# Earlier pooling of v, earlier requests for k, and a reordered first batch in a one-core attention and MLP kernel

## The chip, the cores and the metric

The kernel runs on one core of a Trainium2 chip. The metric is device time in microseconds of one execution. A core has five engines that each take their instructions in order and meet through semaphores: TensorE (PE in the profile, with weight loads as PEld), VectorE (DVE), ScalarE (ACT), GpSimd (POOL) and SyncE (SP), which here issues nearly all DMAs.

## The reference

Two parts, in float32. First an attention in which k and v are averaged over groups of 8 positions, so that 576 queries meet 72 pooled keys; then an MLP with a sine activation over all 8 x 576 = 4608 rows.

```
k_p = k.reshape(B, H, Sp, pool, D).mean(axis=3)        # B, H, S, D = 8, 8, 576, 64; pool = 8, Sp = 72
v_p = v.reshape(B, H, Sp, pool, D).mean(axis=3)
scores = scale * q @ k_p.T ; scores -= max
attn = exp(scores) / (sum + 1e-9)
x = (attn @ v_p) as [4608, 512]
h = x @ w_in                                            # 512 x 2048
g = h + sin(alpha*h)**2 / (alpha + 1e-9)
out = g @ w_out                                         # 2048 x 512
```

## The kernel before

Both matrix products of the MLP are done by Strassen's scheme (seven products for eight). Stage one (`hidden`, matmul at line 770) makes h and g for 512 rows at a time: nine units u = 0 to 8, each of 28 slots, a slot being one of the seven products of one quarter of the columns (four matmuls, 8 records in the trace). g goes to DRAM. Stage two (`outputs`, line 1103) reads g back and makes the output, two levels of Strassen deep.

The attention of batch b = u + 1 is laid between the slots of unit u. `carry(u)` is the written-out plan: `at(slot, f, ...)` puts a call before that slot. All orders are by hand: each engine executes its instructions in the order in which the Python calls issue them, and a DMA request is an instruction in SP's queue. Each DMA has one of eight semaphores in turn, so at most eight are in flight.

What the attention of one batch does in unit u (1 to 6):

- `load_v` (slot 6): two DMAs of 512 KB for the main part of v (512 of 576 rows per head) into a buffer `kvin`, four of 64 KB for the rest into `vr`.
- `two_scores`, `two_shifts` (slots 3 to 6): scores, maximum, subtraction. `exp` on ScalarE (slots 8 to 10). `norm(i)` for four query tiles (slots 9 to 12): a sum and a reciprocal on VectorE, and on GpSimd a multiplication (line 343).
- `turn(i)` (slots 12, 13): VectorE transposes 32 x 32 blocks of the weights into a tile `tr`. `move` (slot 14): sixteen DMAs of 88 or 92 KB (line 487) carry `tr` into `aM`, transposed tile by tile.
- `pool_v` (slot 12): GpSimd adds v's eight neighbours by three halvings (`pool_rows`, line 118), main part, then the rest, then a masked copy (line 137).
- `load_k` (slots 12 and 14, one half of the heads each): one DMA of 576 KB into a `kvin` buffer, and at once its pooling on GpSimd. `kvin` has two buffers, used in turn by v's main part and the two halves of k: a half of k can be requested only when the buffer's last content is pooled. SP's order in slot 14 is: eight moves, second half of k, eight moves.
- `all_values` (slot 25): 44 matmuls (lines 568, 581) of the moved weights with pooled v. They need all moves. `turn_q` (line 209) transposes queries of a later batch into the same `tr`.

Unit 0 has a plan of its own: `load_k(2)` for both halves at slot 17, moves at slot 19, `all_values` at slot 26.

Before slot 0 stands `first_batch`, the attention of batch 0 done in another way, since nothing is there to hide it. Head pairs hp = 0 to 3 go one after the other: `k_head` and `k_last` pool the keys by a matmul with a matrix of ones (`twos`) and copy them from PSUM to `kb2` (`k_last` makes the last 8 of the 72 keys of all heads, from a separately loaded `k_rest`, whose partial sums VectorE adds at lines 148 and 150); `q_head` transposes queries; `products_head` makes scores; `soft_shift`, `soft_exp`, `norm_head` the softmax, the last with two multiplications at line 416 on the engine that it is given; `a_head` transposes the weights, `values` multiplies them with v. `sum_v_rest` and `sum_v_rows` pool v by matmuls (lines 179, 189), copied out by VectorE (line 180) and ScalarE (line 190). `fill(n)` issues n matmuls of ones whose result nobody reads, and line 943 one more of 512 columns. `refine` is four small VectorE operations on the factors of the activation. `self.psum(shape, i)` is PSUM bank i, of eight.

Of the kernel before, what the change touches and what calls it, by code (L numbers as in the profile page):

```python
# [16 lines left out]
OP = mybir.AluOpType  # L17
PSUM = bass.MemoryType.PSUM

P = 128  # L20
POOL = 8
# [19 lines left out]
class Kernel:  # L41
# [61 lines left out]
    def load_k(self, b, e):  # L103

        Sp, D, NP = self.Sp, self.D, self.NP
        m = Sp // 3
        t = self.kvp.tile([P, 2048], F32, name="kvin")[:NP * m, 0:3 * POOL * D]
        self.nc.sync.dma_start(out=t, in_=self.k[b, NP * e:NP * e + NP].rearrange("h (p x) d -> (h p) (x d)", x=3 * POOL))
        if b not in self.kp:
            self.kp[b] = self.ap.tile([NP * m, 3, 2, D], F32, name="kp")  # L110
        t, out = t.rearrange("p (j x) -> p j x", j=3), self.kp[b][:, :, e, :]
        self.pool_rows(t, out)

    def pool_rows(self, t, out):

# [4 lines left out]
    def load_v(self, b):  # L120

        nc, D, H = self.nc, self.D, self.H
        vm, vz = self.vp[b] = self.ap.tile([P, H // 2, D], F32, name="vm", bufs=2), self.ap.tile([P, H // 2, D], F32, name="vz", bufs=2)
        t = self.kvp.tile([P, 2048], F32, name="kvin")[:].rearrange("p (h x) -> p h x", h=4)
        x = self.kvp.tile([P, POOL * D], F32, name="vr", bufs=1)[:]
        for s in range(2):
            nc.sync.dma_start(out=t[64 * s:64 * s + 64],
                              in_=self.v[b, 4 * s:4 * s + 4, 0:4 * P, :].rearrange("h (p t) d -> p h (t d)", t=POOL))
        for s in range(2):
            for c in range(2):  # L130
                r = 64 * s + 32 * c
                nc.sync.dma_start(out=x[r:r + 32], in_=self.v[b, 4 * s:4 * s + 4, 4 * P:, :].rearrange("h (k t) d -> h k (t d)", t=POOL))

        def pool():
            self.pool_rows(t, vm[:])
            self.pool_rows(x, x[:, 0:D])
            nc.gpsimd.tensor_tensor(out=vz[:], in0=x[:, 0:D].unsqueeze(1).to_broadcast([P, H // 2, D]),
                                    in1=self.mask[:].unsqueeze(2).to_broadcast([P, H // 2, D]), op=OP.mult)
        self.pool_v = pool

    def load_k_rest(self, x, out):

        D = self.D
        self.nc.sync.dma_start(out=x, in_=self.k[0, :, 4 * P:, :].rearrange("h (r t) d -> h r (t d)", t=4))
        self.k_rest = out

        def add():
            self.nc.vector.tensor_tensor(out=x[:, 0:2 * D], in0=x[:, 0:2 * D], in1=x[:, 2 * D:4 * D], op=OP.add)
            both = lambda y: y.unsqueeze(1).to_broadcast([P, 2, D])
            self.nc.vector.tensor_tensor(out=out.rearrange("p (u d) -> p u d", u=2), in0=both(x[:, 0:D]), in1=both(x[:, D:2 * D]), op=OP.add)  # L150
        return add

    def load_k_heads(self, hp, dma, eng):
# [25 lines left out]
            nc.tensor.matmul(ps[32 * hp:32 * hp + 32], self.eights[:], self.v_rows[1][:, 2 * hp:2 * hp + 2], start=True, stop=True)  # L179
        nc.vector.tensor_tensor(out=self.vp[b][1][:, 0:2], in0=ps, in1=self.mask[:, 0:2].unsqueeze(2).to_broadcast([P, 2, self.D]), op=OP.mult)  # L180

    def sum_v_rows(self, b, g, i):

        nc = self.nc
        ps = self.psum([P, 2, self.D], i)
        for t in range(4):
            for s in range(2):
                h = 4 * g + 2 * s
                nc.tensor.matmul(ps[64 * s:64 * s + 64], self.twos[:], self.v_rows[0][:, h:h + 2, t, :], start=(t == 0), stop=(t == 3), skip_group_check=True)
        nc.scalar.copy(out=self.vp[b][0][:, 2 * g:2 * g + 2], in_=ps)  # L190
# [37 lines left out]
    def attention(self, b):  # L228
# [125 lines left out]

        def k_last():

            ps = self.psum([P, H, Sp - 64], 4)
            nc.tensor.matmul(ps.rearrange("p h k -> p (h k)"), self.k_rest, self.twos[:], start=True, stop=True)
            nc.vector.tensor_copy(out=self.kb2[:, :, 64:Sp], in_=ps)

# [18 lines left out]

        def products_head(hp):  # L380

            at = 3 if hp % 2 else 5
            self.pair[hp] = ps = self.PS[:, at:at + 2, 0:4 * Sp].rearrange("p u (x k) -> p u x k", x=4)
            for e in range(2):
                for tp in range(2):
                    q = self.qt_tiles(b)[:, hp, 2 * e + tp, :]
                    for r in (0, 64):
                        for u in range(2):
                            s = slice(64 * u, 64 * u + 64)
                            nc.tensor.matmul(ps[r:r + 64, u, 2 * e + tp, :], q[s, r:r + 64], self.kb2[s, 2 * hp + e, :], start=True, stop=True)  # L390
# [133 lines left out]
        def values(hps, banks, n, d):  # L524

            ps = [self.psum([P, 4 * P], i) for i in banks]
            parts = [value_parts(hp, False) for hp in hps]
            for o, (main, _) in zip(ps, parts):
                for e, (w, x) in enumerate(main):
                    nc.tensor.matmul(o[64 * e:64 * e + 64], w, x, start=True, stop=False, skip_group_check=True)  # L530
            for o, (_, (w, x)) in zip(ps, parts):
                nc.tensor.matmul(o, w.rearrange("p e d -> p (e d)"), x, start=False, stop=True, skip_group_check=True)
            if d == 0:
                self.bt[0] = self.home(3, [P, 4, 2, TH])
            turned = [o.rearrange("p (t j) -> p j t", t=4) for o in ps]
            for i in range(n):
                for hp, o in zip(hps, turned):
                    to_x(o, hp, 0, 512 // n * (i + 1), 512 // n * i)
            for kk, o in enumerate(turned):
                y = self.bt[0][:, 0, kk] if d else self.xT[0][:, kk, 0:TH]  # L540
                f = lambda x: x.rearrange("p (j t) -> p j t", t=4)
                nc.vector.scalar_tensor_tensor(out=f(self.bt[0][:, d, kk]), in0=o[:, TH // 4:TH // 2, :], scalar=1.0 / POOL, in1=f(y),  # L542
                                               op0=OP.mult, op1=OP.subtract)

        def values_rest(banks):

# [312 lines left out]
    def first_batch(self):  # L859
# [9 lines left out]
        self.new_q(0)  # L869
        self.load_alpha(self.hp.tile([P, P], F32, name="s", bufs=1)[:])  # L870
        self.load_q_heads(0, 0, 2, nc.scalar)
        add_k = [self.load_k_heads(0, nc.sync, nc.vector)]
        one = self.sm.tile([P, 1], F32, name="one")
        nc.scalar.activation(out=one[:], in_=self.ident[:, 0:1], func=AF.Sqrt)

        def fill(n):

            for _ in range(n):
                nc.tensor.matmul(self.PS[:, 0, 3 * P:4 * P], self.full[:], self.full[:], start=True, stop=True)  # L879
        fill(5)  # L880
        self.turn_alpha()
        refine = self.root()
        nc.scalar.activation(out=one[:], in_=one[:], func=AF.Exp)
# [6 lines left out]
        self.a4 = self.last[:64, 0:512].rearrange("p (j s k) -> p j s k", j=4, s=2)  # L890
        self.z4 = self.last[:64, 512:640].rearrange("p (hp x k) -> p hp x k", hp=4, x=4)
        nc.gpsimd.memset(self.z4, 0.0)
        add_rest = self.load_k_rest(h[1][:, 576:832], far[1][:, 1024:1152])
        for hp in range(1, 4):
            add_k.append(self.load_k_heads(hp, nc.sync, nc.vector if hp < 2 else nc.gpsimd))
            self.load_q_heads(0, 2 * hp, 2 * hp + 2)
# [4 lines left out]
        A.new_a()  # L901
        fill(3)
        A.k_head(0)
        add_rest()
        A.q_head(0)
        A.k_last()
        for f in add_k[1:]:
            f()
        fill(3)
        A.products_head(0)  # L910
        A.k_head(1)
        A.q_head(1)
        A.soft_shift(0)
        A.soft_exp(0)
        refine()
        fill(3)
        A.products_head(1)
        A.k_head(2)
# [2 lines left out]
        A.soft_exp(1)  # L921
        A.norm_head(0, nc.gpsimd)
        A.norm_head(1, nc.vector)
        fill(2)
        A.products_head(2)
        A.k_head(3)
        A.q_head(3)
        self.sum_v_rest(0, 0)
        A.soft_shift(2)
        self.sum_v_rows(0, 0, 2)  # L930
        A.a_head(0, (1, 7, 0))
        self.combine_w_in(0, (0,), nc.gpsimd)
        A.products_head(3)
        A.soft_exp(2)
        A.soft_shift(3)
        A.norm_head(2, nc.gpsimd)
        self.load_q_rest(0, self.q_rest)
        for e in range(2):
            self.load_k(1, e)
        self.load_q(1)  # L940
        self.load_w_in_part(1)
        A.values((0, 1), (5, 6), 2, 0)
        nc.tensor.matmul(self.psum([P, 4 * P], 4), self.full[:], far[0][:, 0:4 * P], start=True, stop=True)
        A.soft_exp(3)
        A.norm_head(3, nc.vector)
        self.combine_w_in(0, (1,))

    def carry(self, u):
# [5 lines left out]
        if u == 0:  # L954
            A0, A = self.att[:2]
            at(1, self.sum_v_rows, 0, 1, 2)
            at(1, A0.rest_q)
            at(1, A0.a_head, 1, (5, 7, 2))
            at(2, A0.values, (2, 3), (2, 1), 1, 1)
            at(2, A0.score, 4)  # L960
            at(2, self.sums_of_x, 0, 2)
            at(2, self.sums_of_x, 0, 3)
            at(2, self.combine_w_in, 0, (2, 3))
            at(2, self.load_w_in_part, 2)
            at(2, self.load_w_in_part, 3)
            at(2, self.pairs_q, 1, range(5))
# [27 lines left out]
            at(9, self.load_q, 2)  # L994
            at(14, self.load_q, 3)
            for e in range(2):
                at(17, self.load_k, 2, e)
            at(27, self.att[2].k_t)
            turn = 23
        else:  # L1000
# [2 lines left out]
        if 0 < u < last:  # L1003
# [10 lines left out]
            at(12, lambda: self.pool_v())  # L1014
            for i in range(2):
                if b < last:
                    at((12, 14)[i], self.load_k, b + 1, i)
            at(14, A.move, 1)
            at(25, A.all_values)
            if b < last:  # L1020
# [217 lines left out]
    def run(self):  # L1238
        nc, tc = self.nc, self.tc
        pool = lambda s, n, b, **kw: s.enter_context(tc.tile_pool(name=n, bufs=b, **kw))  # L1240
        with ExitStack() as top:
# [10 lines left out]
            with ExitStack() as one:  # L1252
# [25 lines left out]
                for s in range(4):  # L1278
                    nc.vector.tensor_reduce(out=self.eights[:, 8 * s:8 * s + 8], in_=x, axis=AX, op=OP.add)
                nc.vector.tensor_reduce(out=self.mask[:], in_=ident[:].rearrange("p (g s k) -> p s g k", s=4, k=8), axis=mybir.AxisListType.XY, op=OP.add)  # L1280
                self.qm, self.qt, self.kp, self.vp, self.pair = {}, {}, {}, {}, {}
                self.bt, self.left, self.group, self.turn = {}, [], None, 2
                self.R = {}
                self.first_batch()
# [64 lines left out]
```

## Time and profile before

| | us |
|---|---|
| median of six runs | 922.42 (919.25 to 924.76) |
| the profiled execution, its own time | 922.5 |
| its span in the trace | 920.6 |
| PE busy in the span | 908.8 |
| first slot of stage one starts at | 23.46 |
| matmul line 568 waiting for the moves or what stands behind them, whole run | 3.0 |

The span is 1.9 us shorter than the time of the same execution, which is within the spread of the runs at their median. In the trace one fp32 matmul leaves two records, a transpose one. A bracket such as [1.07 <-DVE h L841] says that the engine sat idle for 1.07 us just before and which instruction ended that. "SPq" lines are DMA requests on SP; their duration is that of the request, not of the transfer. When a transfer has landed is told by its semaphore's increments.

### The profile page before, as it was taken

What the parts mean: (1) busy time and instruction counts of PE and PEld (TensorE: products, weight loads), DVE (VectorE), ACT (ScalarE), POOL (GpSimd) and SP (SyncE); (2) the same over time, 40 slices, a digit from 0 to 9 for tenths busy, and PEclk for the clock granted to TensorE, in tenths of its full rate; (3) what the DMA queues carried; (4) which work ended last, traced back from release to release, by engine and by line L of the source; (5) the groups of instructions that cost most, each with busy time, mean ns of one, the idle gap of its engine ahead of it and who ended that gap; (6) DMA issues with size and microseconds to landing.
All of it is one profiled execution on the core that took longest, in us unless ns stands there. A gap on an engine that the chain in (4) does not pass through costs nothing.

```text
span 920.6 us, 17757 instructions
## 1 busy us (share of the span) xinstructions
PE 908.8 (99%) x7023; PEld 821.5 (89%) x7023; DVE 662.0 (72%) x1010; ACT 435.8 (47%) x997; POOL 165.0 (18%) x155
## 2 busy tenths in 40 slices
PE   9999999999999999999999999999999999999997
PEld 7787887878878788788888899999999999999997
DVE  6774756747567475673456889988888888979894
ACT  4596675866758667586786631111111112111111
POOL 3875080440704407040000000000000000000000
PEclk9999999999999999999999999999999999999999
DMA  9957765768657656637427237171626253433401
GB/s 260 238 177 199 187 189 175 182 198 198 179 167 181 198 161 170 172 100 244 162 92 245 93 101 229 31 225 30 211 47 184 75 169 90 157 102 120 139 15 39
DMA packets 134731, 141.13 MB, mean 153 GB/s; under 512 B 49832, under 2 KB 103224, under 8 KB 134648
## 3 DMA queue, kind: packets, MB, share of 16 engines
q1 hardware_dynamic: 133304, 138.54, 52.5%
q10 hardware_dynamic: 1344, 1.45, 0.6%
q8 instruction: 56, 0.92, 0.4%
q14 instruction: 27, 0.22, 0.1%
HBM read 75.37 MB, written 47.19 MB: 133 GB/s over the span
## 4 chain that ended last, share of the span: by engine, by line
PE 84%; DMA 5%; DVE 4%; POOL 2%; ACT 1%; issue 1%; SPq 1%; DVEq 0%; POOLq 0%; ACTq 0%
PE PS L1103 41%; PE PS L770 35%; DMA kvin<-in_k_dram 3%; PE PS L568 2%; PE PS L286 2%; DMA q<-in_q_dram 1%; POOL kvin L118 1%; DMA aM<-tr 1%; PE PS L581 1%; DVE tr L209 1%; DVE h L841 1%; PE PS L879 1%; POOL ex L343 1%; ACT s L783 1%; DVE sm L341 1%
## 5 line engine op out<-in xcount | busy, mean ns | idle before, releaser
L770 PE MATMUL PS<-home,a 128*128 128x256 f32 x1152 | 264.1, 381 | 0.6 <-DVE h L749 0.5
L770 PEld LDWEIGHTS PS<-home,a 128*128 128x128 f32 x1152 | 216.7, 190 | 36.4 <-issue 4.8
L770 PE MATMUL PS<-home,as 128*128 128x256 f32 x864 | 200.1, 381 | 0.5 <-DVE home L542 0.5
L770 PEld LDWEIGHTS PS<-home,as 128*128 128x128 f32 x864 | 162.6, 190 | 23.8 <-DVE home L542 0.8
L1103 PE MATMUL PS<-s,wb 128*128 128x144 f32 x896 | 119.3, 286 | 0.4 <-ACT PS L1216 0.4
L1103 PEld LDWEIGHTS PS<-s,wb 128*128 128x128 f32 x896 | 113.7, 190 | 0.7 <-ACT PS L1216 0.6
L783 ACT ACTIVATE s<-s,c 128x256 f32<-128x256 f32 (+1 forms) x216 | 110.0, 572 | 0.0
L749 DVE TENSOR_TENSOR h<-PS,p 128x512 f32<-128x512 f32 x72 | 49.2, 684 | 78.6 <-PE PS L770 36.4
L776 ACT ACTIVATE s<-h,al 128x256 f32<-128x256 f32 x144 | 65.1, 503 | 55.4 <-DVE h L749 54.6
L1216 ACT COPY PS<-PS 128x144 f32<-128x144 f32 x56 | 14.7, 263 | 145.7 <-PE PS L1103 144.3
L776 ACT ACTIVATE s<-PS,al 128x256 f32<-128x256 f32 x144 | 59.9, 467 | 38.9 <-PE PS L770 20.0
L343 POOL TENSOR_TENSOR ex<-ex,sm 128x576 f32<-128x576 f32 (+1 forms) x28 | 35.0, 1269 | 214.5 <-ACT PS L810 200.9
L1103 PE MATMUL PS<-s,a 128*128 128x144 f32 x512 | 73.2, 286 | 0.0
L1103 PE MATMUL PS<-r,wb 128*128 128x144 f32 x512 | 73.2, 286 | 0.0
L841 DVE TENSOR_TENSOR h<-PS,s 128x512 f32<-128x512 f32 x36 | 24.7, 686 | 64.4 <-ACT s L783 64.4
L118 POOL TENSOR_TENSOR kvin<-kvin 96x768 f32<-96x768 f32 (+3 forms) x42 | 66.1, 1573 | 13.2 <-DMA kvin<-in_k_dram 8.4
L1103 PEld LDWEIGHTS PS<-r,wb 128*128 128x128 f32 x512 | 67.1, 190 | 0.1
L1103 PEld LDWEIGHTS PS<-s,a 128*128 128x128 f32 x512 | 67.0, 190 | 0.0
L1235 ACT COPY PS<-PS 128x144 f32<-128x144 f32 x56 | 14.7, 263 | 88.5 <-PE PS L1103 88.5
L1103 PE MATMUL PS<-s,we 128*128 128x144 f32 x384 | 54.9, 286 | 0.0
L1103 PE MATMUL PS<-x,wb 128*128 128x144 f32 x384 | 54.9, 286 | 0.0
L1103 PEld LDWEIGHTS PS<-s,we 128*128 128x128 f32 x384 | 50.3, 190 | 0.1
(191 smaller groups left out, 1216.9 us busy)
## 6 DMA issues: line engine op xcount, KB each, us to landing
g_bridge<-h SPq DMA_DIRECT2D x72, 512.0 KB
r<-g_bridge SPq DMA_DIRECT2D x31, 1152.0 KB
out_dram<-o SPq DMA_DIRECT2D x128, 72.0 KB
kvin<-in_k_dram SPq DMA_DIRECT2D x14, 576.0 KB
q<-in_q_dram SPq DMA_DIRECT2D x7, 1024.0 KB
kvin<-in_v_dram SPq DMA_DIRECT2D x14, 512.0 KB
aM<-tr SPq DMA_DIRECT2D x56, 92.0 KB
aM<-tr SPq DMA_DIRECT2D x56, 88.0 KB
```

Of the source, the lines that this page charges most:

```text
L118: self.nc.gpsimd.tensor_tensor(out=t[..., 0:w] if w > D else out, in0=t[..., 0:w], in1=t[..., w:2 * w], op=OP.add)
L286: nc.tensor.matmul(ps[e][r0 + r:r0 + r + q.shape[-1], h, :], q[s], kb[s, hp, :], start=True, stop=True)
L343: nc.gpsimd.tensor_tensor(out=E(i), in0=E(i), in1=sm.unsqueeze(2).to_broadcast([P, n, Sp]), op=OP.mult)
L568: nc.tensor.matmul(o[r:r + 64], w, x, start=start and i < 2, stop=False, skip_group_check=True)
L749: add = lambda o, x, y: nc.vector.tensor_tensor(out=o, in0=x, in1=y, op=OP.add)
L770: nc.tensor.matmul(ps[:, jj, :], self.A[p][:, kk, f * P:(f + 1) * P], x[:, kk, :], start=(start and jj == 0 and kk == 0), stop=(kk == 1), ...
L776: nc.scalar.activation(out=G.s[:, i, jj, j, :], in_=src[:, jj], func=AF.Sin, scale=self.al[:, f:f + 1])
L783: nc.scalar.activation(out=x, in_=x, func=AF.Square, scale=self.c[:, f:f + 1])
L841: add = lambda o, x, y: self.nc.vector.tensor_tensor(out=o, in0=x, in1=y, op=OP.add)
L1103: nc.tensor.matmul(out, W[:, J // 2, J % 2, :], A[:, J, :], start=(start and J == 0), stop=(J == self.NJ - 1), skip_group_check=True)
L1216: nc.scalar.copy(out=x1[:, 0, :], in_=x0[:, 1, :])
L1235: nc.scalar.copy(out=x1[:, 1, :], in_=x1[:, 0, :])
```

## The change

It has two parts.

In units 0 to 6: the main part of v is pooled by `load_v` itself, so its three GpSimd additions stand in GpSimd's queue at slot 6 (slot 7 in unit 0), ahead of the four `norm`, while the rest stays at slot 12. `load_k` only requests; the pooling is kept in `pool_k` and called apart. Both halves of k are requested at slot 12, ahead of all moves (in unit 0 also at slot 12, with their pooling left at slot 17).

In the first batch and unit 0: `k_rest` is requested first on SP and summed on GpSimd; `k_last` comes straight after `k_head(0)`, in bank 2; the fillers are fewer (one of 512 columns and one of 128 for five, two for three, none for two and for line 943); `sum_v_rest` and `sum_v_rows` stand ahead of `products_head(2)` and write two column ranges of bank 0, where `sum_v_rows` wrote bank 2; `products_head` of odd pairs uses banks 2 and 3 instead of 3 and 4; `refine` comes later; `norm_head(3)` is on GpSimd instead of VectorE, ahead of the pooling of k; in `values(2, 3)` VectorE's differences come ahead of ScalarE's copies; two VectorE combinations of w_in come one slot earlier.

```diff
 def load_k(self, b, e):
...
-        self.pool_rows(t, out)
+        self.pool_k[e] = lambda: self.pool_rows(t, out)
 def load_v(self, b):
...
+        self.pool_rows(t, vm[:])
         def pool():
-            self.pool_rows(t, vm[:])
             self.pool_rows(x, x[:, 0:D])
 def load_k_rest(self, x, out):
...
-            self.nc.vector.tensor_tensor(out=x[:, 0:2 * D], ...)
+            self.nc.gpsimd.tensor_tensor(out=x[:, 0:2 * D], ...)
-            self.nc.vector.tensor_tensor(out=out.rearrange(...), ...)
+            self.nc.gpsimd.tensor_tensor(out=out.rearrange(...), ...)
-    def sum_v_rows(self, b, g, i):
+    def sum_v_rows(self, b, g, i, c=0):
-        ps = self.psum([P, 2, self.D], i)
+        ps = self.PS[:, i, c:c + 2 * self.D].rearrange("p (h d) -> p h d", h=2)
 def k_last():
-            ps = self.psum([P, H, Sp - 64], 4)
+            ps = self.psum([P, H, Sp - 64], 2)
 def products_head(hp):
-            at = 3 if hp % 2 else 5
+            at = 2 if hp % 2 else 5
 def values(hps, banks, n, d):
+            if d:
+                differences()          # the two scalar_tensor_tensor of VectorE
             for i in range(n): ... to_x(...)
-            for kk, o in enumerate(turned): (the same two)
+            if not d:
+                differences()
 def first_batch(self):
         self.load_q_heads(0, 0, 2, nc.scalar)
+        add_rest = self.load_k_rest(h[1][:, 576:832], far[1][:, 1024:1152])
         add_k = [self.load_k_heads(0, nc.sync, nc.vector)]
...
-        fill(5)
+        nc.tensor.matmul(self.psum([P, 4, P], 4), self.full[:], self.full[:].unsqueeze(1).to_broadcast([P, 4, P]), start=True, stop=True)
+        fill(1)
...
-        add_rest = self.load_k_rest(h[1][:, 576:832], far[1][:, 1024:1152])
+        add_rest()
...
         A.k_head(0)
-        add_rest()
+        A.k_last()
         A.q_head(0)
-        A.k_last()
...
-        fill(3)
+        fill(2)
         A.products_head(0)
...
-        refine()
...
         A.norm_head(1, nc.vector)
-        fill(2)
+        self.sum_v_rest(0, 0)
+        self.sum_v_rows(0, 0, 0, 128)
         A.products_head(2)
         A.k_head(3)
         A.q_head(3)
-        self.sum_v_rest(0, 0)
+        refine()
         A.soft_shift(2)
-        self.sum_v_rows(0, 0, 2)
         A.a_head(0, (1, 7, 0))
...
+        A.values((0, 1), (5, 6), 2, 0)
+        A.soft_exp(3)
+        A.norm_head(3, nc.gpsimd)
         self.load_q_rest(0, self.q_rest)
         for e in range(2):
             self.load_k(1, e)
+            self.pool_k[e]()
...
-        A.values((0, 1), (5, 6), 2, 0)
-        nc.tensor.matmul(self.psum([P, 4 * P], 4), self.full[:], far[0][:, 0:4 * P], start=True, stop=True)
-        A.soft_exp(3)
-        A.norm_head(3, nc.vector)
 def carry(self, u):
+            at(1, self.combine_w_in, 0, (2, 3))
-            at(2, self.combine_w_in, 0, (2, 3))
...
-                at(17, self.load_k, 2, e)
+                at(12, self.load_k, 2, e)
+                at(17, lambda e=e: self.pool_k[e]())
...
-                    at((12, 14)[i], self.load_k, b + 1, i)
+                    at(12, self.load_k, b + 1, i)
+                    at(12, lambda i=i: self.pool_k[i]())
```

## The prediction

> **What bounds the kernel now.** I read the busy shares and the chain that ended last first, then TensorE's timeline wherever it stood still, then the DMA requests.
>
> ```profile
> PE 908.8 (99%) x7023; PEld 821.5 (89%) x7023; DVE 662.0 (72%) x1010; ACT 435.8 (47%) x997; POOL 165.0 (18%) x155
> PE 84%; DMA 5%; DVE 4%; POOL 2%; ACT 1%; issue 1%; SPq 1%; DVEq 0%; POOLq 0%; ACTq 0%
> ```
>
> TensorE is busy 908.8 of 920.6 us. The matmuls of the two stages are not edited, so a gain can come from two places only: TensorE's holes, and its work before the first slot. The waits of the line that uses the moves come next (whole run, columns: total, times, longest), then the holes' surroundings, from the timelines of SyncE's requests, TensorE and GpSimd.
>
> ```profile
> PE PS L568 <- DVE h L841: 1.6, 3, 1.1
> PE PS L568 <- DMA aM<-tr: 1.4, 1, 1.4
> ...
> 72.13 11.28 SPq L487 DMA_DIRECT2D aM<-tr  x16
> 85.12 0.65 PE L568 MATMUL PS<-aM,vm 64*64 64x512 f32 x6 [1.39 <-DMA aM<-tr]
> ...
> 237.67 5.98 SPq L487 DMA_DIRECT2D aM<-tr  x8
> 243.75 0.52 SPq L108 DMA_DIRECT2D kvin<-in_k_dram  x1
> 244.32 5.42 SPq L487 DMA_DIRECT2D aM<-tr  x8
> 252.41 2.37 DVE L209 STREAM_TRANSPOSE tr<-q 128x1024 f32<-128x1024 f32 x2 [6.38 <-DMA aM<-tr]
> 255.41 0.33 PE L568 MATMUL PS<-aM,vm 64*64 64x64 f32 x4 [1.07 <-DVE h L841]
> ...
> 409.21 10.12 SPq L487 DMA_DIRECT2D aM<-tr  x16
> ```
>
> Unit 0 waits for the moves themselves. In unit 3 (and, smaller, 1 and 5) the delay is passed on: the query transposes of line 209 reuse `tr`, so they wait for the last move, line 841 stands behind them on VectorE, and line 568 needs line 841's bank. The three such holes are 0.20, 1.07 and 0.37 us. Units 2, 4, 6 show none. The last batch, which has no k to load, is the undisturbed row: its moves landed at 420.85, 11.64 us after the first request.
>
> The start, on TensorE and VectorE:
>
> ```profile
> 12.56 0.73 PE L390 MATMUL PS<-h,q 64*64 64x72 f32 x32
> 14.23 0.71 PE L879 MATMUL PS<-full 128*128 128x128 f32 x4
> 15.00 0.73 PE L390 MATMUL PS<-h,q 64*64 64x72 f32 x32
> 16.69 0.42 PE L179 MATMUL PS<-p,eights 64*32 64x128 f32 x8
> 17.44 1.09 PE L189 MATMUL PS<-h,twos 128*64 128x128 f32 x16 [0.32 <-ACT q L370]
> 22.50 1.13 PE L943 MATMUL PS<-home,full 128*128 128x512 f32 x2
> ...
> 4.40 0.36 DVE L160 TENSOR_TENSOR home<-home 128x256 f32<-128x256 f32 x1
> 16.71 1.07 DVE L416 TENSOR_TENSOR tr<-ex,sm 128x512 f32<-128x512 f32 x2
> 17.71 0.28 DVE L180 TENSOR_TENSOR vz<-PS,mask 128x128 f32<-128x128 f32 x1
> 33.12 0.91 DVE L542 SCALAR_TENSOR_TENSOR home<-PS,home 128x256 f32<-128x256 f32 x2 [4.04 <-ACT home L501]
> ```
>
> VectorE's copy of `sum_v_rest` (line 180) starts 5.15 us after `products_head(1)` (12.56), because it stands behind the division of pair 1 (line 416). Nothing waits for that now: `sum_v_rows` writes another bank.
>
> **Moves, part by part.** Both halves of k now go ahead, so the sixteen moves are requested in one piece and I price them with the undisturbed 11.64 us. Unit 0: first request 72.13, landed 84.92 today (k held requests for 0.8 us); then 83.77. TensorE waited 1.39 us and would go on about 0.2 after the landing, 83.97 against 85.12: gain 1.15. Unit 1: 123.94 to 137.64 today, then about 135.6; unit 3: 237.67 to 252.09, then 249.3; unit 5: 352.08 to 365.96, then 363.7. Each is 2 us or more earlier, against holes of 0.20, 1.07 and 0.37: all 1.64 us go. Together 1.15 + 1.64 = **-2.8 us**. What is late next in unit 0 is the moves still; in the others TensorE's own order.
>
> What this may cost. The pooling of v's main part (at unit 3: additions of 236.16 to 239.97 and a last one of 1.65 us, some 5.5 us in all) now stands in front of the softmax multiplications on GpSimd. V's main part landed at 111.2, 167.5, 225.6, 282.4, 337.7 and 394.9 in units 1 to 6, and the first multiplication started at 115.2, 172.2, 229.0, 287.0, 343.3 and 400.5: 3.4 to 5.6 us later. So the multiplications come 0 to 2.2 us later, most in unit 3; the turns, 2.6 us behind the first multiplication, by up to 1.1. Unit 3's moves would then land at 250.4, still 1.7 ahead of today against a hole of 1.07: no cost. On SyncE the second k request now waits until v is pooled (116.5 in unit 1, by 111.2 + 5.3); nothing but k and the moves of 123.94 stands behind it there. GpSimd beside VectorE slows it: line 841 took 2.30 beside pooling in unit 0 and 1.22 without. The cover is ScalarE's finishing of a bank 2.2 us before its slot; without it, one such step per unit, at most 6 x 1.1 = 6.6 us; at the other end nothing. I take nothing, since the same pooling stood beside the same work of later slots and TensorE shows no hole there.
>
> **The start, part by part.** Up to `products_head(1)`. `k_rest` is requested ahead of pair 0's keys; its request took 0.81 us. These keys landed at 3.60; by that shift alone 4.4, and by the row of pair 1's keys (requested 2.12, landed 6.67, so 4.55) up to 6.1. VectorE's addition started at 4.40 straight after other work, so the loss lies between 0 and 1.6; I take 0.65 (keys at about 5.0, nearer the shift, since little else is in flight). `k_last` without its wait and two fillers in place of three shorten the stretch from `k_head(0)` (5.28) to `products_head(0)` (9.31) from 4.03 to about 3.45, by 0.55. Net +0.1, between -0.5 and +1.0.
>
> From `products_head(1)`, time T. Now TensorE does `k_head(2)`, `q_head(2)` (12.56 to 14.23: 1.67) and `sum_v_rest` (0.42): it is at `sum_v_rows` at T + 2.09. In the changed program that matmul writes the bank which line 180's copy reads, and it waits for that copy, in VectorE's order still behind the division: T + 5.15 + 0.28 + 0.06 = T + 5.49. **TensorE stands still 3.40 us.** Behind it wait, in order: `sum_v_rows` 1.02 (17.44 to 18.46), `products_head(2)` 0.66 and `k_head(3)`, `q_head(3)` 1.03 (15.00 to 16.69), `a_head(0)` 1.47 (18.46 to 19.93), `products_head(3)` and `values` 2.57 (19.93 to 22.50). Sum 6.75, then some 0.3 for ScalarE's copies, which the filler of line 943 used to cover. Slot 0 at T + 12.54, against T + 10.90 (23.46). Loss **1.64**. Fillers are part of that sum already: 3.40 - 0.77 (two of 128) - 0.96 (line 943) - 0.32 (wait on ScalarE) + 0.3.
>
> Slot 2: TensorE waited 0.49 there for VectorE's differences, which now precede ScalarE's copies: -0.45. The last division goes to GpSimd, 1.30 to 1.74 us for its two multiplications against 2.37 on VectorE: the wait of 0.32 before `a_head(1)` stays about as it is. Behind that division GpSimd starts pooling k some 4 us later; it had 3.21 us without work at 43.7 and the second pooling is wanted at 38.09, so I charge nothing; uncovered, about 1 us. `refine` (four VectorE instructions, 0.7 us) lands where VectorE waits for the late `products_head(2)`; the two combinations (0.68 each) in its 4.04 us of idle time before slot 2. Start: 0.1 + 1.64 - 0.45 = **+1.3 us**.
>
> [...]
>
> **Sum.** 922.5 (profiled execution; the median is 922.4) + 1.3 - 2.8 = **921.0**.
>
> **The rivals.**
> 1. The start doesn't lose. Without the 3.40 us wait TensorE would only meet GpSimd's division of pair 0 (ends 17.70), about 0.4 us: 1.64 - 3.40 + 0.4 - 0.45 + 0.1 = -1.7, so 918.0. If pair 1's softmax reaches VectorE sooner, half of it: 919.5. For it: the wait hangs on VectorE's order alone. Against: lines 416 and 180 above follow without idle time.
> 2. The moves land no earlier, set by the later turn and by both halves of k in flight beside them. Then 922.5 + 1.3 = 923.8. Against: 1.7 us of room in unit 3.
> 3. Slower: TensorE's clock falls in the standstill. The granted clock:
>
> ```profile
> 914.00:918.00 4.00, 1.17 (x10) 0.95 (x8) 1.98 (x4) 0.00 (x0) 0.00 (x0) 1.00 0.46 98
> 918.00:921.00 3.00, 0.00 (x0) 0.00 (x0) 0.00 (x0) 0.00 (x0) 0.00 (x0) 0.68 0.30 65
> ```
>
> It fell at 919.09, 3.9 us after the last matmul (915.2). The standstill of 3.4 is nearly that. At the start the rate doubled only at 11.15, 10.1 us after the first matmul (six records of line 879 took 1.59 us at 7.79, 0.83 at 11.72). Some 10 us at half rate, 90% busy, cost 4.5: 921.0 + 4.5 = 925.5. It decides from 9 us at half rate on; today's longest hole after 11.15 is 1.55 and shows no fall.
> [...]
>
> **How the numbers follow.** A measurement of this kernel can tell about 0.3%, 2.8 us: faster is below 919.65, slower above 925.2. Chances: the forecast 0.50 (own range 919.7 to 922.8, from the keys' -0.5 to +1.0 and a hole or two that stays), rival 1 0.30, rival 2 0.10, rival 3 0.10. Faster: rival 1 and a little of the forecast's edge, 0.32. Slower: rival 3 and the tail of rival 2, 0.12. Same: 0.56. The range reaches from rival 1's lower end, 918.0, to 924.4, above rival 2, leaving out rival 3 and part of rival 1.
>
> **What would show it.** Right: a hole of about 3.4 us on TensorE at 15 to 18 us with `sum_v_rows` waiting for line 180's successor on VectorE; slot 0 at about 25.2; sixteen moves in one group in each unit; no wait of line 568 for line 841 in units 1, 3, 5, and one of about 0.2 for the moves in unit 0. Wrong: slot 0 before 24; a granted clock below 1 after 18 us; new waits of slots for ScalarE's or VectorE's steps in slots 6 to 12, where v's pooling now stands; or moves still landing over 12.5 us after their first request.

## The result, and the profile after

The changed kernel takes 918.47 us (median of 21 runs, 916.4 to 919.8), the kernel before 921.87 (47 runs). The ratio is 0.9958, 95% interval 0.9949 to 0.9968: faster by 0.42%, 3.9 us (the medians differ by 3.4), where 1.5 was forecast. The small difference hides two larger errors of opposite sign. In the profiled execution (919.1 us, span 917.2) slot 0 of stage one starts 4.41 us later than before, and the last matmul of stage one still comes 3.40 us earlier. So the start lost far more than forecast, and the moves gained far more.

The page of the changed kernel, busy shares and the chain that ended last. Lines of the file moved by one to nine: 568 is now 575, 841 is 848, 770 is 777, 180 is 181.

```profile
PE 904.0 (99%) x7009; PEld 821.0 (90%) x7009; DVE 665.1 (73%) x1006; ACT 435.6 (47%) x997; POOL 169.3 (18%) x159
PE 96%; DVE 1%; DMA 1%; issue 0%; ACT 0%; SPq 0%; POOL 0%; DVEq 0%; ACTq 0%; POOLq 0%
```

The chain is now TensorE alone almost throughout; DMA, VectorE and GpSimd had 11% of it. TensorE's busy time fell by 4.8 us, 4.4 of them behind the start of slot 0 (ahead of it TensorE was busy 22.0 and 21.6 us), although no matmul is gone there: busy time of before contained waiting.

**The start.** TensorE's timeline of the changed kernel:

```profile
13.63 0.73 PE L391 MATMUL PS<-h,q 64*64 64x72 f32 x32
...
15.32 0.42 PE L180 MATMUL PS<-p,eights 64*32 64x128 f32 x8
19.18 1.57 PE L190 MATMUL PS<-h,twos 128*64 128x128 f32 x16 [3.44 <-DVE vz L181]
20.68 1.24 PE L391 MATMUL PS<-h,q 64*64 64x72 f32 x32
...
27.87 1.99 PE L777 MATMUL PS<-home,a 128*128 128x256 f32 x8 [0.47 <-ACT home L502]
```

The standstill of 3.44 us stands where it was forecast (3.40), for the reason that was forecast. But `sum_v_rows` behind it takes 1.57 us where 1.09 was shown before, and `products_head(2)` 1.24 for 0.73. The windows of the changed kernel tell why. The granted clock is the share of its full clock that TensorE got (columns: stretch, its length, busy time and count of PE, PEld, DVE, ACT and POOL, granted clock, DMA share, GB/s):

```profile
19.00:19.50 0.50, 0.32 (x6) 0.32 (x8) 0.50 (x2) 0.00 (x0) 0.50 (x1) 1.00 1.08 258
19.50:20.00 0.50, 0.50 (x12) 0.50 (x8) 0.50 (x1) 0.00 (x0) 0.50 (x1) 0.65 1.01 234
20.00:20.50 0.50, 0.50 (x8) 0.35 (x4) 0.43 (x3) 0.00 (x0) 0.07 (x1) 0.50 0.97 221
...
22.50:23.00 0.50, 0.50 (x5) 0.50 (x5) 0.47 (x2) 0.00 (x0) 0.00 (x0) 0.50 0.09 37
23.00:23.50 0.50, 0.50 (x6) 0.50 (x5) 0.50 (x1) 0.27 (x1) 0.00 (x0) 0.94 0.03 12
```

The granted clock fell to 0.50 at about 19.65, 3.9 us after TensorE had stopped (15.74), when TensorE was already at work again, and stayed there for 3.4 us. From `products_head(1)` to slot 0 it is 14.24 us instead of 10.90.

**The moves.** The time from the last slot before `all_values` to the first after it, read from the starts of the matmuls, in us:

| unit | 0 | 1 | 2 | 3 | 4 | 5 | 6 |
|---|---|---|---|---|---|---|---|
| before | 5.56 | 5.11 | 4.91 | 5.98 | 4.49 | 5.28 | 3.72 |
| changed | 4.22 | 4.52 | 3.72 | 4.16 | 3.72 | 3.72 | 3.72 |

Unit 6 has no k to load, and shows what the stretch takes undisturbed. The others were 9.0 us above it in sum and are now 1.7 above. The prediction counted only what TensorE's idle brackets say, 2.8 of their 3.0 us. Where the rest was, unit 2 shows, in which the prediction found no hole. TensorE (with one of its weight loads) and VectorE of the kernel before:

```profile
194.58 2.37 DVE L209 STREAM_TRANSPOSE tr<-q 128x1024 f32<-128x1024 f32 x2 [5.31 <-DMA aM<-tr]
196.87 0.65 DVE L841 TENSOR_TENSOR h<-PS,s 128x512 f32<-128x512 f32 x1
...
196.51 1.40 PE L568 MATMUL PS<-aM,vm 64*64 64x512 f32 x8
...
197.58 0.19 PEld L568 LDWEIGHTS PS<-aM,vm 64*64 64x64 f32 x4 [0.88 <-DVE h L841]
...
197.75 0.28 PE L568 MATMUL PS<-aM,vz 64*64 64x64 f32 x4
```

and TensorE of the changed kernel in the same unit:

```profile
198.42 0.65 PE L575 MATMUL PS<-aM,vm 64*64 64x512 f32 x6
198.60 0.28 PE L575 MATMUL PS<-aM,vz 64*64 64x64 f32 x4
```

These are matmuls of 64 x 64 weights, and groups of them run side by side on TensorE here (198.42 to 199.07 and 198.60 to 198.88). After the change the 64-column group for the last queries starts 0.2 us after the first 512-column group and runs beside it. Before, it starts 1.24 us after: its bank is read until 197.52 (196.87 + 0.65) by line 841, which stood behind line 209, which had waited for the moves. TensorE was never idle, since the first group was running, but it ran alone for over a microsecond. No idle bracket of PE shows that; the waits of the weight loads do. The waits of PEld of the kernel before (total, times, longest):

```profile
PEld PS L568 <- DVE h L841: 5.6, 5, 1.9
...
PEld PS L568 <- DVE order L575: 1.6, 5, 0.3
```

The first row is 1.09, 0.88, 1.95, 0.46 and 1.25 us in units 1 to 5, and in each of them the stretch is longer than the undisturbed one by 0.3 us more than that (1.39, 1.19, 2.26, 0.77, 1.56). The second row, a wait of 0.33 us for a one-column copy (line 575) of the same late group's bank, stands in these five units and not in unit 6. The two rows make 7.2 us, as much as the five stretches are too long. The 1.6 us of idle PE for line 841 lie within the first row's waits, and aren't added.

### The profile page after: what moved, and what is told of

Same layout as the page of the kernel before. It is cut to its first block, busy times and chain, and to the rows that moved or that the text cites. A ratio compares the mean times of both kernels' runs of the same rounds, so it can differ in the third digit from the quotient of the medians.

```text
span 917.2 us, 17735 instructions
## 1 busy us (share of the span) xinstructions
PE 904.0 (99%) x7009; PEld 821.0 (90%) x7009; DVE 665.1 (73%) x1006; ACT 435.6 (47%) x997; POOL 169.3 (18%) x159
## 4 chain that ended last, share of the span: by engine, by line
PE 96%; DVE 1%; DMA 1%; issue 0%; ACT 0%; SPq 0%; POOL 0%; DVEq 0%; ACTq 0%; POOLq 0%
PE PS L777 47%; PE PS L1112 41%; PE PS L287 2%; PE PS L575 2%; PE PS L588 1%; DMA home<-in_k_dram 0%; PE PS L391 0%; PE PS L353 0%; PE PS L370 0%; DVE sm L411 0%; PE PS L533 0%; PE PS L260 0%; PE PS L249 0%; PE PS L445 0%; PE PS L531 0%
## 5 line engine op out<-in xcount | busy, mean ns | idle before, releaser
L118 POOL TENSOR_TENSOR kvin<-kvin 96x768 f32<-96x768 f32 (+3 forms) x42 | 70.2, 1671 | 194.0 <-DMA kvin<-in_v_dram 192.4
L1112 PEld LDWEIGHTS PS<-x,wb 128*128 128x128 f32 x384 | 50.3, 190 | 0.0
```

Source lines behind the costliest of these rows:

```text
L118: self.nc.gpsimd.tensor_tensor(out=t[..., 0:w] if w > D else out, in0=t[..., 0:w], in1=t[..., w:2 * w], op=OP.add)
L1112: nc.tensor.matmul(out, W[:, J // 2, J % 2, :], A[:, J, :], start=(start and J == 0), stop=(J == self.NJ - 1), skip_group_check=True)
```

## The experiments

Each was timed against the kernel before on the same chip; times are medians, ratios go with their 95% intervals.

**1. The first part of the change alone.** The kernel before with the diff of `load_k`, `load_v`, `pool_rows` and of `carry`'s `load_k` lines.

```diff
+        self.pool_rows(t, vm[:])
         def pool():
-            self.pool_rows(t, vm[:])
...
-                    at((12, 14)[i], self.load_k, b + 1, i)
+                    at(12, self.load_k, b + 1, i)
+                    at(12, lambda i=i: self.pool_k[i]())
```

> The kernel before with only the first part of the change (v's main part pooled by its load, both halves of k requested ahead of the moves, units 0 to 6). Theory A: the delay of the moves cost more than TensorE's visible holes, because line 568's second group of matmuls waited for VectorE's line 841 while the first group ran, and so lost the running side by side; the stretch from the last slot before all_values to the first after it shrinks in units 0 to 5 from 5.56, 5.11, 4.91, 5.98, 4.49, 5.28 us to about 4.2, 4.5, 3.7, 4.2, 3.7, 3.7, as in the changed kernel. Gain 7.3 us, so 914.6. Theory B, the prediction's: only the holes go, gain 2.8 us, so 919.1; the rest of the shorter stretches in the changed kernel came from the first batch's shift of phase.

Measured: 915.66 us, ratio 0.9942 (0.9921 to 0.9963). The stretches are 4.37, 3.72, 3.72, 3.97, 3.72, 4.27 us. Theory A holds for them, 7.6 us less than before, and theory B falls. Part of it was given back in this execution: its slot 0 came at 21.47 and TensorE then waited for the combined input weights of slot 4.

```profile
PE PS L771 <- DVE a L642: 1.9, 1, 1.9
```

That is a wait that neither the kernel before nor the changed one shows, where these weights are combined in time for a later slot 0 or one slot earlier.

**2. The second part alone.** The changed kernel with the first part taken back.

```diff
-        self.pool_rows(t, vm[:])
         def pool():
+            self.pool_rows(t, vm[:])
...
-                    at(12, self.load_k, b + 1, i)
-                    at(12, lambda i=i: self.pool_k[i]())
+                    at((12, 14)[i], lambda i=i: (self.load_k(b + 1, i), self.pool_k[i]()))
```

> The kernel before with only the second part of the change (the first batch, with unit 0's combinations one slot earlier). Theory A: slot 0 starts at 27.9 instead of 23.5, slot 2 gets 0.5 back, and the stretches around all_values stay as before: loss 3.9 us, so 925.8. Theory B: part of the lateness is taken up again in unit 0, whose moves then wait less, loss under 3 us: below 924.9.

Measured: 926.65 us, ratio 1.0052 (1.0031 to 1.0073): slower, as theory A has it. The new first batch costs about 4.8 us, and the stretches stay as long as before (5.79, 4.91, 5.19, 5.76, 4.64, 5.56). The two parts alone add up to no gain within their intervals, -0.58% and +0.52%, the whole change gives -0.42%. Some of that difference lies in the intervals of 0.2% each, some perhaps in the wait of experiment 1; how much of each is open. One more part is seen in experiment 2's profiled execution: the standstill is there too (3.12 us), but the granted clock was 0.50 from 15.81 to 22.64, 6.8 us for 3.4 (its mean over the execution was 0.995 for 0.996), and from `products_head(1)` to slot 0 it took 15.43 us, 1.19 more than in the changed kernel. Slot 0 came at 26.61, not at 27.9 as expected, since `products_head(1)` started at 11.18. How often executions of either kernel have the longer fall is not known.

**3. `sum_v_rows` in a bank of its own.**

```diff
-        self.sum_v_rows(0, 0, 0, 128)
+        self.sum_v_rows(0, 0, 4)
```

> The changed kernel with sum_v_rows in bank 4, which nothing uses there, so that it waits for no copy of VectorE. Theory A: the standstill of 3.44 us goes and with it the fall of the granted clock at 19.6, worth another 1.5 us; some 0.4 us come back as a wait for GpSimd's division before a_head(0). Gain 4.5 us, so 914.0, slot 0 near 23.4. Theory B: the clock falls all the same, or the softmax of pair 2 is late next: gain 3 us or less, 915.5 or more.

Measured: 915.76 us, ratio 0.9934 (0.9913 to 0.9956), 2.7 us below the changed kernel. The standstill and the fall of the clock are gone (`sum_v_rows` starts at 15.87 and takes 1.09 us, `products_head(2)` 0.73; from `products_head(1)` to slot 0 11.46 us, after 14.24), but a new wait took 1.5 us of it, so the gain is theory B's size. TensorE's waits of this kernel (total, times, longest):

```profile
PE PS L531 <- DVE ex L399: 1.5, 1, 1.5
```

and VectorE's timeline:

```profile
19.05 0.28 DVE L181 TENSOR_TENSOR vz<-PS,mask 128x128 f32<-128x128 f32 x1
19.25 1.07 DVE L617 TENSOR_TENSOR t<-c 128x16 f32<-128x16 f32 x1
...
20.77 0.17 DVE L617 TENSOR_TENSOR c<-c,t 128x16 f32<-128x16 f32 x1
20.86 0.75 DVE L397 TENSOR_REDUCE mx<-PS 128x8 f32<-128x576 f32 x1
```

`values(0, 1)` needs the bank that `soft_shift(2)` reads, and this now stands behind `refine` (line 617 and 618), which the change had moved there. With the standstill `refine` cost nothing; without it, 1.5 us. The outputs of this kernel and of experiment 4's are wrong (relative error 0.087 and 0.084). Both write only a part of bank 4 shortly before stage one, whose third product adds to what ScalarE copied there, and that is the likely cause: experiment 5 writes all of bank 4, experiment 9 uses bank 7, and their outputs are right. Wrong values don't change which instructions run, and the two right kernels show the same effects, the one of the filler and the one of another bank, so the times can be used.

**4 and 5. TensorE kept busy during the standstill.** The wait stays; matmuls of ones stand before it, eight of 128 columns or two of 512.

```diff
         self.sum_v_rest(0, 0)
+        for _ in range(8):
+            nc.tensor.matmul(self.PS[:, 4, 3 * P:4 * P], self.full[:], self.full[:], start=True, stop=True)
         self.sum_v_rows(0, 0, 0, 128)
```

> The changed kernel with eight matmuls of ones of 128 columns, into bank 4, between sum_v_rest and sum_v_rows: the wait for VectorE's copy stays, but TensorE works during it. Theory A: what lies behind the standstill ran at half rate from 19.6 to 23.0 because TensorE had stood still; with the filler the granted clock stays 1.00, and 1.5 us come back, so 917.0; slot 0 near 26.3. Theory B: the fall has another cause (or comes from the power of later work), no change: 918.5. By the prediction's price of a fall, 4.5 us, it would be 914.0.

```diff
+        for _ in range(2):
+            nc.tensor.matmul(self.psum([P, 4, P], 4), self.full[:], self.full[:].unsqueeze(1).to_broadcast([P, 4, P]), start=True, stop=True)
```

> The changed kernel with two matmuls of ones of 512 columns between sum_v_rest and sum_v_rows, the whole of bank 4 each time as at the start: the wait for VectorE's copy stays, TensorE works during most of it. Theory A: no fall of the granted clock at 19 to 20 us; from products_head(1) to slot 0 12.7 us (as in e4_filled_wait) instead of 14.2: 917.0. Theory B: no change, 918.5.

Measured: 917.33 us (ratio 0.9952, 0.9936 to 0.9968) and 916.67 (0.9937, 0.9914 to 0.9959); from `products_head(1)` to slot 0 12.69 and 12.70 us. TensorE's timeline of the second:

```profile
15.62 1.98 PE L933 MATMUL PS<-full 128*128 128x512 f32 x4
19.14 1.09 PE L190 MATMUL PS<-h,twos 128*64 128x128 f32 x16 [1.53 <-DVE vz L181]
```

and its window from 20 to 21 us, with the columns as above:

```profile
20.00:21.00 1.00, 1.00 (x40) 0.76 (x34) 0.62 (x5) 0.27 (x1) 0.03 (x1) 1.00 0.91 246
```

`sum_v_rows` waits for the same copy and starts as late, 5.56 us after `products_head(1)` for 5.55, but takes 1.09 us, and the clock stays at 1.00. The filler doesn't cover all of the standstill; 1.53 us of it are left. So the fall came from the standstill and cost 14.24 - 12.70 = 1.54 us. The medians of the whole runs, 1.1 and 1.8 us lower, agree, but their intervals alone would not show it.

**6. The query transposes moved behind `all_values`.** The kernel before, with nothing of the change:

```diff
-                at(turn + part, self.turn_q, u + 2, part)
+                at((25, 25, 26, 27)[part] if u else turn + part, self.turn_q, u + 2, part)
```

> The kernel before with one thing moved: in units 1 to 5 the query transposes of line 209 come after all_values (slots 25 to 27 instead of 22 to 25), so that line 841 no longer stands behind them on VectorE. The moves land as late as before. Theory A (the late moves cost time only through line 209 and line 841, most of it as matmuls that do not run side by side): the stretches around all_values shrink from 5.11, 4.91, 5.98, 4.49, 5.28 us to 3.7 to 4.5 although no move is earlier; gain 5.5 to 7.2, so 915 to 916.6. Unit 0 keeps its 5.56. Theory B (all_values is bound by the landing of the moves): gain under 1 us, above 921.

Measured: 914.77 us, ratio 0.9922 (0.9907 to 0.9937), 7.2 us faster, more than the whole change. The stretches of units 1 to 5 are all 3.72. Unit 3, where k's second half is still requested between the moves and the last one landed 14.2 us after the first request, as before (14.4), on VectorE and TensorE:

```profile
248.08 0.69 DVE L841 TENSOR_TENSOR h<-PS,s 128x512 f32<-128x512 f32 x1 [4.81 <-ACT s L783]
...
252.14 3.02 DVE L209 STREAM_TRANSPOSE tr<-q 128x1024 f32<-128x1024 f32 x4 [0.21 <-issue]
...
250.51 0.65 PE L568 MATMUL PS<-aM,vm 64*64 64x512 f32 x6
250.69 0.28 PE L568 MATMUL PS<-aM,vz 64*64 64x64 f32 x4
```

This settles it: in units 1 to 5 the late moves never held TensorE themselves, only through line 209 and line 841. The stretches of these units lost 7.2 us, which is what the two rows of PEld's waits add up to, and neither row is among this kernel's waits. (Unit 0's stretch was 4.23 here against 5.56; nothing was edited there, but slot 0 came 1.5 us later in this execution, and the moves landed at 84.89, as before (84.92), so TensorE waited less for them.)

**7. Only v pooled early.** The kernel before with `load_v` alone changed.

```diff
+        self.pool_rows(t, vm[:])
         def pool():
-            self.pool_rows(t, vm[:])
```

> The kernel before with only v's main part pooled by its load; the second half of k is still requested between the two eights of moves, and unit 0's k at slot 17. Theory A: what makes the moves late is the 0.5 us request of k between them, the semaphores it takes and its 576 KB in flight beside them, not the pooling: moves land within 0.5 us of before, gain under 1 us, above 921. Theory B: the pooling of v held k and through it the moves: the moves of units 1, 3, 5 land 2 us earlier, gain over 3 us, below 919.

Measured: 922.41 us, ratio 1.0007 (0.9991 to 1.0024): no gain. Stretches 5.25, 4.84, 5.88, 4.32, 5.55 in units 1 to 5. The early pooling brings nothing, and a cost doesn't show within the interval; it only allows what brings the gain, the earlier request of k's second half. Unit 0's stretch was 7.88 in this execution, not 5.56: slot 0 came 1.1 us earlier and the moves landed at 84.31, so TensorE waited 2.22 us for them, and the granted clock fell to 0.50 from 85.66 to 89.08.

**8. The keys of pair 0 first.** The changed kernel with the order of before for these two requests.

```diff
-        add_rest = self.load_k_rest(h[1][:, 576:832], far[1][:, 1024:1152])
         add_k = [self.load_k_heads(0, nc.sync, nc.vector)]
+        add_rest = self.load_k_rest(h[1][:, 576:832], far[1][:, 1024:1152])
```

> The changed kernel with the keys of pair 0 requested ahead of k_rest again. Theory A: k_head(0) starts at 5.3 instead of 6.6 and the rest of the first batch with it, less some 0.5 for k_last, which then waits for k_rest: gain 0.8, so 917.7. Theory B: k_last, now straight after k_head(0), is held by k_rest as long as the keys were: no change, 918.5.

Measured: 917.35 us, ratio 0.9951 (0.9936 to 0.9967), 1.1 us below the changed kernel's median, but the intervals overlap; theory A is likely and not shown.

**9. All three mends of the start.** `sum_v_rows` in bank 7, `refine` back behind `soft_exp(0)`, the keys first.

```diff
...
-        self.sum_v_rows(0, 0, 0, 128)
+        self.sum_v_rows(0, 0, 7)
...
         A.soft_exp(0)
+        refine()
...
         A.q_head(3)
-        refine()
```

> The changed kernel with sum_v_rows in bank 7 (read out long before), refine back behind soft_exp(0), where VectorE waits for TensorE, and the keys of pair 0 requested first. In e3_free_bank a wait of 1.47 us of values(0, 1) for VectorE's soft_shift(2) took the place of the standstill, because the division of pair 1, line 181 and the four of refine stood before it. Theory A: without refine there that wait falls to some 0.1 us: slot 0 about 1.5 earlier than in e3_free_bank and 0.8 for the keys: 913.5. Theory B: ScalarE's exponential or GpSimd's division of pair 2 is late next, and what slot 0 gains is lost before slot 2 or at the first slots that wait for w_in: 915.5.

Measured: 913.38 us, ratio 0.9912 (0.9896 to 0.9928). From `products_head(1)` to slot 0 it takes 9.76 us, 1.1 less than in the kernel before. Theory A. So the new order of the start is shorter than the old one, once nothing waits behind it. That the earlier sums of v are what helps is not shown: the matmuls without a reader that are gone from this stretch, two of 128 columns and line 943, took 0.77 and 0.96 us of it before, more than the 1.1 us.

**10, 11 and 12. Both remedies together.** Experiment 9 with experiment 6's edit:

> e8_bank_refine_keys with the query transposes of line 209 behind all_values in units 1 to 5 as well. Theory A: what is left over 3.72 us around all_values in units 1 to 5 of e8_bank_refine_keys (0, 0, 0.34, 0, 0.72) goes: gain 1.0, so 912.4. Theory B: those are other waits: 913.4.

912.44 us, ratio 0.9902 (0.9876 to 0.9929); stretches of units 1 to 5 all 3.72. The same with v's pooling and k's second half in units 1 to 6 as in the kernel before:

```diff
-        self.pool_rows(t, vm[:])
         def pool():
+            self.pool_rows(t, vm[:])
...
-                    at(12, self.load_k, b + 1, i)
+                    at((12, 14)[i], lambda i=i: (self.load_k(b + 1, i), self.pool_k[i]()))
```

> e9_all_and_late_turn_q with the first part of the change taken back in units 1 to 6: v's main part is pooled at slot 12, the second half of k requested between the two eights of moves. Theory A: once line 841 doesn't stand behind line 209, the time at which the moves land no longer matters in these units: same as e9_all_and_late_turn_q within 0.5 us, 912.4, stretches of 3.7. Theory B: the moves land too late for all_values itself in some units: 914 or more.

913.27 us, ratio 0.9903 (0.9878 to 0.9928): the same. Unit 3's requests in this kernel are again split,

```profile
232.16 6.06 SPq L487 DMA_DIRECT2D aM<-tr  x8
238.32 0.52 SPq L108 DMA_DIRECT2D kvin<-in_k_dram  x1
238.89 5.64 SPq L487 DMA_DIRECT2D aM<-tr  x8
```

and its stretches are still 3.72 or 3.73. So in units 1 to 6 the first part of the change cures a symptom; the order on VectorE was the cause. Last, the first of these three kernels (v and k as changed) with `k_last` behind `q_head(0)` again:

```diff
         A.k_head(0)
-        A.k_last()
         A.q_head(0)
+        A.k_last()
```

> e9_all_and_late_turn_q with k_last behind q_head(0), as in the kernel before. Theory A: the 0.56 us for which k_last waits for k_rest on GpSimd is covered by q_head(0): 911.9. Theory B: k_last then delays products_head(0) by its copy, as before the change: no gain, 912.4 or more.

911.90 us, ratio 0.9887 (0.9865 to 0.9910), the fastest of the study; the step from 912.44 alone is within the intervals. What is waited for next is shown by TensorE's waits of this kernel: unit 0's `all_values`, now that slot 0 comes at 20.8, waits for its moves again.

```profile
PE PS L575 <- DMA aM<-tr: 1.0, 1, 1.0
```

## Why the prediction was wrong, point by point

- **What the moves gain: wrong in size, the step that failed.** The mechanism was right: moves in one piece, line 209, line 841, bank of line 568. The term was mis-sized: the step "Each is 2 us or more earlier, against holes of 0.20, 1.07 and 0.37: all 1.64 us go" took PE's idle brackets for the whole price. With unit 0's 1.15 it made 2.8 us. The stretches shrank by 7.3 us (1.34, 0.59, 1.19, 1.82, 0.77 and 1.56 in units 0 to 5). "Units 2, 4, 6 show none" was the wrong sentence: 2 and 4 lost 1.19 and 0.77 us as matmuls that ran alone instead of side by side. The numbers that would have said it were in the trace: 5.6 us of PEld's waits for line 841, and unit 6's undisturbed 3.72.
- **When the moves land: right in units 0, 2 and 4, too early in 1, 3 and 5.** Estimated 11.64 us after the first request. In the changed kernel it is 11.6 to 11.7 us in units 0, 2 and 4, but 13.1, 12.6 and 12.3 in units 1, 3 and 5, two of them over the 12.5 that the prediction named as a sign of being wrong. K's two halves were requested ahead of the moves in all six, so they alone don't explain it. In unit 3 one of the sixteen requests took 1.58 us where the others took about 0.59; what held it is open. Units 1 and 3 so kept 0.80 and 0.44 us.
- **The early pooling of v at no cost: right as far as experiment 7 can tell** (ratio 1.0007, 0.9991 to 1.0024).
- **The standstill: right**, 3.44 us against 3.40, with the waiter, the releaser and the place named. The matmul and the copy use different columns of one bank, and the matmul waited for the copy all the same; a bank of its own (experiment 3) took the wait away.
- **From `products_head(1)` to slot 0: 12.54 forecast, 14.24 measured.** With TensorE kept busy it is 12.70, so the sum was right but for the clock. This was rival 3's mechanism, which was given 1 in 10 and a price of 4.5 us from the slow clock's 10.1 us at the start. It happened, and cost 1.54 us: the clock came back after 3.4 us (19.65 to 23.06), so the nearest row of the trace was too high. The fall came 3.9 us after the stop, as at the end of the kernel before. The prediction took a standstill of 3.4 us as short enough beside those 3.9; the fall arrived although work had resumed in between (at 19.18), and falls came after standstills of 3.12 us (experiment 2), 2.22 (experiment 7) and 1.55 (experiment 4, as the last section shows) too. (The longest hole after 11.15 in the kernel before is 1.39 us, at 85.12, not 1.55.)
- **Up to `products_head(1)`: +0.1 forecast, +1.07 in the profile.** The keys' addition started at 5.70, not at about 5.0. But single profiles can't settle this term, as told below.
- **Slot 2: -0.45 forecast, -0.56 measured** from slot 1 to slot 2. **The division on GpSimd:** a wait of 0.55 instead of 0.32 before `a_head(1)`, so slot 1 starts 0.3 us later after slot 0; with both, slot 2 is 4.14 us later than before.
- **The sum.** Start +1.3 forecast, slot 2's gain included; +4.1 at slot 2 in the profile, +4.8 by the median of experiment 2. Moves -2.8 forecast, -7.3 in the stretches and -6.5 by the median of experiment 1. Errors of 2.8 and 4.5 us of opposite sign in the profiles left some 2 us in the total. The result lies near rival 1's 918.0 and so inside the outer range (918.0 to 924.4). That is luck: rival 1 held that the start doesn't lose, and the start lost more than forecast.

## What to carry to other kernels

Price a disturbed stretch by the time from the last instruction before it to the first after it, against an undisturbed repetition of the same stretch, not by the idle time of the busiest engine: where small matmuls run side by side, a late bank cost time here in which TensorE counts as busy, and the waits of its weight loads, 5.6 us, showed it. When several engines wait in a row (transfer, transposes, an addition, a matmul), look for the one that needn't be in the row: moving it by two or three slots gave 7.2 us, as much as hurrying the transfer did. And before an instruction is moved ahead on TensorE, look for who last reads its bank and what stands before that reader; if a standstill must be, fill a part of it (two matmuls of 512 columns left 1.53 us of 3.44, and the clock stayed at 1.00).

## What the runs showed of the hardware

The time from TensorE's stop to a fall of the granted clock was not the same each time: 3.9 us at the end of the kernel before (915.16 to 919.09) and at the changed one's standstill (15.74 to 19.65), 2.2 us (911.76 to 913.94) at the changed one's end. In each of these two traces the times at which the clock changes lie whole multiples of 3.413 us apart: in the changed kernel 19.65, 23.06 and 913.94 are 1 and 261 such lengths apart, in the kernel before 11.15, where the rate doubled, and 919.09 are 266.

The length of a standstill alone didn't decide in these runs. After one of 1.85 us the four matmuls of a slot took 1.97 us (experiment 1, at 38.96), about the 1.89 of the slot at 34.09, and after one of 1.55 us a fall is seen (experiment 4). These are the 3.41 us ahead of the changed kernel's fall, a stretch as long of experiment 4, ahead of its `products_head(1)`, and one of experiment 5 (columns as above):

```profile
16.24:19.65 3.41, 0.47 (x8) 0.47 (x10) 3.31 (x8) 0.53 (x1) 2.55 (x3) 1.00 1.14 253
...
5.56:8.97 3.41, 1.83 (x18) 1.64 (x19) 2.06 (x6) 1.26 (x3) 0.45 (x2) 1.00 1.03 346
...
16.16:19.57 3.41, 1.88 (x12) 0.81 (x12) 3.31 (x8) 0.56 (x1) 2.51 (x3) 1.00 1.13 270
```

TensorE was busy 14%, 54% and 55% of them. Behind the first the clock was 0.50 for 3.4 us. Behind the second, with the standstill of 1.55 us, four transposes of queries (line 370) took 1.06 us at 10.97, after 0.61 at 7.63, and 0.61 again at 14.02. Behind the third, with 1.53 us of standstill, the clock stayed at 1.00. Ahead of the fall at the changed kernel's end (910.53 to 913.94) TensorE was busy 36%; in the kernel before, 59% (82.83 to 86.24, with the hole of 1.39 us) were followed by no fall. What decides between these cases is not shown.

The first rise of the rate came at different times too. With the same start, the kernel before transposed pair 0's queries in 1.06 us and experiment 1 in 0.61:

```profile
6.19 1.06 PE L369 MATMUL PS<-ident,q 128*128 128x128 f32 x4
```

```profile
5.77 0.61 PE L370 MATMUL PS<-ident,q 128*128 128x128 f32 x4
```

`products_head(1)` then started at 12.56 and 10.57, and in experiments 6 and 7, which share that start too, at 13.85 and 11.43: over 3 us between executions. That is about half as much as the kernel's runs differ by (919.25 to 925.94), and why a term of a microsecond in the start has to be read from medians, or from a point behind the rise.
